# First six chunks' scores from each head's own 40 rows, the two heads of a pair by turns

## The chip, the cores and the metric

The kernel runs on one core of one Trainium2 chip. The metric is the device time of one execution in microseconds (us); lower is better. Engines are called as in the profile: PE is TensorE's matmul, PEld its weight load, DVE is VectorE, ACT is ScalarE, POOL is GpSimd, SP is SyncE, which here issues DMAs.

## The reference

A gated linear recurrence per head (batch 4, 8 heads, 768 steps, head size 40) and a feed-forward layer over all 3072 tokens:

```python
for t in range(S):
    m_new = np.maximum(f_gate[:, :, t] + m, i_gate[:, :, t])
    f_stab = np.exp(f_gate[:, :, t] + m - m_new)
    i_stab = np.exp(i_gate[:, :, t] - m_new)
    C = f_stab * C + i_stab * np.einsum('bhd,bhe->bhde', vt, kt)
    n = f_stab * n + i_stab * kt
    h_tilde = np.einsum('bhde,bhe->bhd', C, qt)
    denom = np.maximum(np.abs(np.einsum('bhd,bhd->bh', n, qt)), 1.0)
    y[:, :, t] = sigmoid(o_gate[:, :, t]) * h_tilde / denom
...
x = y.transpose(0, 2, 1, 3).reshape(3072, 320)
h = x @ w_in                                    # 320 -> 2048
g = np.maximum(h, 0) + alpha * np.minimum(h, 0)
out = g @ w_out                                 # 2048 -> 320
```

## The kernel before

**Tiling.** Each batch's 768 steps are cut into six chunks of 128, so there are 24 chunks `n` in all; two chunks make a group `g` of 256 tokens, 12 groups, and the feed-forward layer runs group by group. Inside a chunk the recurrence becomes attention-like products: scores `pS` = keys times queries, weighed by decays `E`, times values (`pH`), plus the part from the running state `C` (`pI`); the state is then updated (`pu`). The first six chunks (batch 0) work in f32, the later ones on split bf16 parts; the change touches only the first six.

**How the first six chunks' scores are made.** Queries and keys are loaded by token (`qn`, `kn`), eight heads of 64 columns each, of which 40 hold data and the rest zeros. A transpose of two heads at once (`pqk`, step `qT` for queries and `kT` for keys) puts head 2p on partitions 0 to 39 and head 2p+1 on partitions 64 to 103 (`R` is 104). ACT copies queries to `qf` (step `qc`). Keys go into `kf`, a tile with two halves (step `kc`, two copies, L329 and L330): half 0 holds only the even heads' rows and half 1 only the odd heads'; the other rows are cleared once by POOL (step `kfz`, L318 and L319). A score product then runs over all 104 rows, and the cleared rows take the other head out. The step `sc{n}{par}` does the four heads of one parity of chunk n into one bank of PSUM; `wg{n}{par}` (L1096, DVE) multiplies with the decays.

**What sets the order.** `ORDER` is a list of step names that is emitted in this order; each engine and the whole program are pinned to it. Names that matter here: `sp`/`sq` spread a row of logs over partitions (`pb`), `ex`/`ey` make decays on ACT, `v` is the product with values, `fm`/`ft` the part from the state, `ta` adds, `gr gg gx gp` gate the result into `xn`, `x` transposes it to channels, `xa`/`xd` split it into XH (ACT) and XL (DVE), `um`/`uc` update the state. `i..`, `r..`, `o..` load and split weights of the feed-forward layer (last letters: d DMA, s and x on ACT, y and j on DVE, h on ACT, l on DVE, p on POOL). `U R S G K` with group and pair are the up-product, relu, slope, high part and low part of the feed-forward layer (small `r s g` and V, N the variant for other pairs), `D` the down-product. `warm2` is a pair of filler matmuls. The later part of the program follows `PATTERN`, which does not change.

Of the kernel before, what the change touches and what calls it, by code (L numbers as in the profile page):

```python
# [8 lines left out]
F32 = mybir.dt.float32  # L9
# [8 lines left out]
def kernel(ctx: ExitStack, tc: tile.TileContext, q, k, v, i_gate, f_gate, o_gate, w_in, w_out, alpha, out):  # L18
    nc = tc.nc
    B, H, S, D = q.shape  # L20
    DM, DFF = w_in.shape
    P = 128
# [3 lines left out]
    GC = 2  # L26
# [142 lines left out]
    def weighed(n):  # L169

        b, c = divmod(n, NC)
        kd = sb.tile([P, H, D], F32, tag="kd", name=f"kd{n}")
        (nc.gpsimd if n in KDP else nc.vector).tensor_tensor(
            kd, by_token_of(n, 1), wT[:, c, b * H : (b + 1) * H].unsqueeze(2).broadcast_to([P, H, D]), ALU.mult
        )
        kds[n] = kd
# [135 lines left out]
    kpads = []

    def padded_tiles():


        for K in kpads:
            nc.gpsimd.memset(K[64:R, 0], 0.0)  # L318
            nc.gpsimd.memset(K[:64, 1], 0.0)  # L319

    def zero_states():
        for C in C_t:
            nc.gpsimd.memset(C, 0.0)

    def padded(n):
        return kpads[(n + NDIR) % 2]

    def padded_copy(K, pk):
        nc.scalar.copy(K[:64, 0], pk[:64])  # L329
        nc.scalar.copy(K[64:R, 1], pk[64:R])  # L330
# [308 lines left out]
    def row_of(g, fp, e):  # L639
# [5 lines left out]
    NDIR = 6  # L645
# [7 lines left out]
    ORDER = """warm14 dq0 Cz warm2 warm2 warm2 qT0 warm2 sca0 lf0a kT0 i00d lf0z lf0b li0 L0 sca1 bj0 dq1 warm2 qc0 lqa lqb kc0 lqc lqd sp01 eeL i00s
        lf1a lqe wt0 warm2 warm2 warm2 qT1 qc1 bTt bTc ex01 warm2 sp00 warm2 warm2 sp11 r0d lf1b ewj wTt wTc ex00 warm2
        sp10 ex11 kT1 i00y L1 li1 do0 dv0 kfz i01d eTt ex10 wd0 dq2 gma i00j sc00 o0d lpa sc01 um0 kc1 gmd gmm sc11
        eTc eel bj1 og1 r0s uc0 fm1 wtl wg01 sc10 ewl lpb i11d wd1 alT wg00 gmc qT2 i01s glt ft1 wg10 glc alC dL lpc
        lpd lpe qc2 warm2 wg11 dv1 um1 uc1 i00h i01x i01j kT2 kc2 i00p o0s o0x sp20 v0 r0y r0j gr0 sp21 fm2 dq3 ex20
        warm2 o0j r0h i01h ft2 i01p ex21 o0h warm2 gg0 r0l gx0 i11s sc20 wg20 v1 ta1 gr1 qT3 qc3 i11x gp0 x0 xa0 sc21
        dL4 gg1 gx1 gp1 kT3 wg21 x1 xa1 o1d wd3 xd0 r0H xd1 wd2 sq30 ey30 r0L i11j ex40 o0l F0 U00 i20d i10d R00 S00
        kc3 v2 ta2 um2 uc2 o1s o1y U01 dq4 i10s i10x i10j sq31 gr2 o1j i11k i11l ey31 qT4 G00 ex41 fm3 ft3 sc30 K00  # L660
        wg30 i10h um3 uc3 D00 R01 kT4 i20s do1 S01 qc4 wd4 kc4 o1h i20x sc31 wg31 dv2 um4 uc4 i20j og2 o2d i20h gg2
        i10p fm4 o1l o5d sc41 wg41 G01 K01 i21d gx2 r2d sc40 i20p o2s o2x dq5 wg40 o5s o5x v3 ta3 o2j gr3 gg3 o2h o5j
        r2s dL5 o4d r2x o2l U02 o3d r2j gx3 gp3 R02 gp2 i21s v4 ft4 ta4 qT5 qc5 r2H ex50 r2h r2p U03 x2 R03 S02 G02 x3
        dq6 i21y i21j r2L i31d fm5 ft5 xa2 xd2 i21h i21p dv3 i30d kT5 kc5 K02 S03 o4s o4y D01 G03 wd6 K03 o3s o3y o3j
        D02 do2 dL7 ex51 o7d o4j o6d U04 R04 S04 o3h xa3 V05 r05 o3p o4h sc50 o4p sc51 G04 i31s i31x xd3 s05 wg51 um6
        uc6 K04 gr4 wg50 F1 U10 U11 R10 S10 og3 gg4 gx4 dL6 gp4 R11 S11 G10 o5h o5p v5 K10 D10 U12 ta5 G11 g05 K11 vp0
        i31j i30s i30x gr5 gg5 U13 i31h i30j R12 i30h D11 S12 i31l G12 gx5 gp5 K12 D12 R13 dq7 S13 o7s i30l U06 o7x
        do3 o7j N05 G13 K13 D13 tp0 o6s tp1 o6x R06 tp2 x4 x5 o6j o6h vp1 U07 o7h tp3 D03 D04 D05 R07 S06 G06 S07 o6l
        xa5 xd5 xa4 xd4 G07 K06 K07 D06 o7l D07 Z0"""
# [271 lines left out]
    def first_group():  # L941
# [14 lines left out]
        f, i, rst, m = fi[:, 0, :S], fi[:, 1, :S], rm[:, 0, :S], rm[:, 1, : S + 1]  # L956
# [54 lines left out]
            nc.vector.tensor_copy(gates[:, GC:], ps[:, : (NC - GC) * n].rearrange("p (c a) -> p c a", a=n))  # L1011
            yield

        for j in range(2):
            kpads.append(sb.tile([P, 2, 512], F32, tag="kS", name=f"kf{j}", bufs=2))
        qk = {}

        def by_channel(n, j, copy):
            pq = psa(f"pqk{n}_{j}")
            transposed(pq, (qn_t if j == 0 else kn_t)[n % NQ])  # L1020
            yield
            if j == 0:
                qk[n] = sb.tile([P, 512], F32, tag="qf", name=f"qf{n}"), padded(n)
# [56 lines left out]

        pS = {}

        def scores(n, par):
            if n >= GC:
                ps = psa(f"pS{n}_{par}")
            elif n * par == 0:
                ps = ps_h.tile([P, 512], F32, tag="h", name=f"pS{n}_{par}")
            else:
                ps = ps_o.tile([P, 512], F32, tag="o1", name=f"pS{n}_{par}")
            for p in range(NPR):  # L1090
                sl = slice(p * P, (p + 1) * P)
                nc.tensor.matmul(ps[:, sl], qk[n][1][:R, par, sl], qk[n][0][:R, sl], start=True, stop=True)  # L1092
            pS[n, par] = ps

        def weigh(n, par):
            nc.vector.tensor_tensor(E[n, par], pS[n, par], E[n, par], ALU.mult)  # L1096
# [34 lines left out]
        steps = {}  # L1131
# [55 lines left out]
        def decay_parts(k, tag):  # L1187
# [25 lines left out]
            bj1=lambda: nc.gpsimd.tensor_tensor(bj[:, t1], li[:, t1], L[:, t1], ALU.subtract),
# [9 lines left out]
        def values_of(n):  # L1223
            got["h", n] = values(n, [E[n, 0], E[n, 1]])
# [5 lines left out]
        def chunk_steps(n):  # L1230

            steps[f"wd{n}"] = lambda: weighed(n)
            steps[f"v{n}"] = lambda: values_of(n)
            steps[f"ta{n}"] = lambda: added(n)
            steps[f"x{n}"] = lambda: x_first(n)
            add(f"xa{n} xd{n}", lazily(lambda: x_parts(n)))
            add(f"um{n} uc{n}", lazily(lambda: update_steps(n)))
            if n > 0:
                add(f"fm{n} ft{n}", lazily(lambda: state_part(n)))
            add(f"gr{n} gg{n} gx{n} gp{n}", lazily(lambda: gated_steps(n, got["T" if n else "h", n])))  # L1240
            add(f"qT{n} qc{n}", lazily(lambda: by_channel(n, 0, nc.scalar.copy)))
# [123 lines left out]
```

## Time and profile before

| what | value |
|---|---|
| median of 3 runs (lowest, highest) | 456.08 us (455.85, 456.25) |
| the profiled execution | 456.2 us, span 454.5 us, granted clock 0.998 |
| busy share PE, DVE, ACT, POOL | 99%, 68%, 69%, 69% |
| score matmuls of the first six chunks (L1092) | 96, starting between 14.2 and 67.2 us |
| copies into `kf` (L329 and L330) | 12, starting between 7.0 and 60.8 us |

The table's shares are means over the whole span. The change lies in the first 70 us or so, where the six chunks of batch 0, the gates' scans and the splitting of all weights run beside the first feed-forward products; a busy PE there includes modelled ends of matmuls, so how far apart two groups start says more than how long they are shown busy.

### The profile page before, as it was taken

The numbers are of one execution on the slowest core, as the hardware profiler recorded it, in microseconds if no ns is written. First come the engines' busy times: TensorE is split into PE (matmuls) and PEld (weight loads), VectorE is DVE, ScalarE is ACT, GpSimd is POOL, SyncE is SP. The second block draws the span as 40 slices with busy tenths as digits, with TensorE's granted clock in tenths as the row PEclk, the third lists the DMA queues.
The fourth block names the chain that finished last, engine by engine and source line by source line (L and its number), as shares of the span: only waits on it lengthen the run. The fifth ranks groups of instructions, "written<-read, shape, count | busy, mean of one in ns | idle before, by whom it ended". The sixth has DMA issues, their size and how long they took to land.

```text
span 454.5 us, 11766 instructions
## 1 busy us (share of the span) xinstructions
PE 448.2 (99%) x4418; PEld 438.8 (97%) x4418; DVE 310.9 (68%) x659; ACT 314.9 (69%) x717; POOL 312.6 (69%) x400
## 2 busy tenths in 40 slices
PE   8999999999999999999999999999999999999996
PEld 6789999999999999999999999999999999999996
DVE  4798999558866767767767767767767767753321
ACT  5999997959767767758768758658758668433331
POOL 7836566737889698588798698597798696143231
PEclk9999999999999999999999999999999999999999
DMA  8999998769674575597783783589682451000000
GB/s 182 248 253 214 232 232 226 139 143 180 156 168 110 137 160 104 133 184 163 121 183 103 131 179 105 115 188 180 128 168 86 97 142 40 1 30 1 30 1 29
DMA packets 156162, 61.60 MB, mean 136 GB/s; under 512 B 140154, under 2 KB 145834, under 8 KB 156106
## 3 DMA queue, kind: packets, MB, share of 16 engines
q1 hardware_dynamic: 156026, 60.75, 59.9%
q8 instruction: 35, 0.57, 0.5%
q14 instruction: 21, 0.17, 0.1%
q10 hardware_dynamic: 80, 0.11, 0.1%
HBM read 36.90 MB, written 4.03 MB: 90 GB/s over the span
## 4 chain that ended last, share of the span: by engine, by line
PE 91%; ACT 4%; DVE 3%; POOL 1%; issue 1%; POOLq 0%; DVEq 0%; ACTq 0%
PE po L771 36%; PE ph L734 5%; PE ph L739 5%; PE ph L735 5%; PE ph L736 5%; PE ph L741 5%; PE ph L737 5%; PE ph L740 5%; PE ph L738 5%; PE pH L390 4%; PE pS L491 4%; PE pu L192 2%; PE px L600 2%; PE pS L1092 2%; PE pH L349 2%; PE pI L415 1%
## 5 line engine op out<-in xcount | busy, mean ns | idle before, releaser
L760 POOL TENSOR_TENSOR gl<-g,gh 128x512 fp32r<-128x512 f32 x74 | 96.1, 1301 | 32.5 <-ACT gh L758 31.3
L744 ACT ACTIVATE g<-ph 128x512 f32<-128x512 f32 x96 | 57.3, 597 | 81.7 <-PE ph L741 79.7
L771 PE MATMUL po<-OH,gh 128*128 128x320 f32 x368 | 111.3, 314 | 0.0
L771 PE MATMUL po<-OL,gh 128*128 128x320 f32 x368 | 108.7, 308 | 0.0
L749 DVE SCALAR_TENSOR_TENSOR g<-g,oma,ph 128x256 f32<-128x256 f32 x148 | 63.6, 471 | 65.5 <-ACT g L744 64.1
L771 PEld LDWEIGHTS po<-OH,gh 128*128 128x128 f32 x368 | 69.2, 188 | 0.0
L771 PEld LDWEIGHTS po<-OL,gh 128*128 128x128 f32 x368 | 69.2, 188 | 0.0
L771 PE MATMUL po<-OH,gl 128*128 128x320 f32 x368 | 68.8, 308 | 0.0
L771 PEld LDWEIGHTS po<-OH,gl 128*128 128x128 f32 x368 | 57.5, 188 | 0.3 <-DVE gl L760 0.3
L734 PE MATMUL ph<-XH,WH 128*128 128x256 f32 x192 | 54.1, 282 | 0.5 <-DVE g L749 0.5
L735 PE MATMUL ph<-XH,WH 128*128 128x256 f32 x192 | 53.4, 278 | 0.0
L736 PE MATMUL ph<-XH,WL 128*128 128x256 f32 x192 | 53.2, 277 | 0.0
L739 PE MATMUL ph<-XL,WH 128*128 128x256 f32 x192 | 53.2, 277 | 0.0
L741 PE MATMUL ph<-XL,W 128*128 128x256 f32 x192 | 53.1, 277 | 0.0
L737 PE MATMUL ph<-XH,WL 128*128 128x256 f32 x192 | 53.1, 277 | 0.0
L738 PE MATMUL ph<-XH,W 128*128 128x256 f32 x192 | 53.1, 276 | 0.0
L740 PE MATMUL ph<-XL,WH 128*128 128x256 f32 x192 | 53.1, 276 | 0.0
L462 ACT ACTIVATE E<-Lb,gates 128x128 f32<-128x128 f32 x160 | 50.0, 393 | 0.0
L758 ACT CAST gh<-g 128x512 fp32r<-128x512 f32 x74 | 45.7, 618 | 4.0 <-PE po L771 2.4
L375 ACT CAST E<-pS 128x512 bf16<-128x512 f32 x72 | 41.1, 582 | 6.3 <-DVE pS L372 5.8
L465 POOL TENSOR_SCALAR_AFFINE_SELECT E<-E 128x512 f32<-128x512 f32 x40 | 27.0, 676 | 15.0 <-ACT E L462 14.4
L734 PEld LDWEIGHTS ph<-XH,WH 128*128 128x128 f32 x192 | 36.1, 188 | 0.6 <-ACT gh L758 0.6
(200 smaller groups left out, 1127.2 us busy)
## 6 DMA issues: line engine op xcount, KB each, us to landing
Lb<-L_d SPq DMA_DIRECT2D x20, 512.0 KB
wo<-in_moe_w_out_dram SPq DMA_DIRECT2D x8, 640.0 KB
wi<-in_moe_w_in_dram SPq DMA_DIRECT2D x8, 512.0 KB
qn<-in_q_dram SPq DMA_DIRECT2D x24, 160.0 KB
kn<-in_k_dram SPq DMA_DIRECT2D x24, 160.0 KB
og<-in_o_gate_dram SPq DMA_DIRECT2D x24, 160.0 KB
va<-in_v_dram SPq DMA_DIRECT2D x24, 160.0 KB
out_dram<-ob SPq DMA_DIRECT2D x11, 320.0 KB
```

The costliest lines, as they stand in the source:

```text
L734: nc.tensor.matmul(dst, WH[half][:, 0, hs], XH[:, 0], start=True, stop=False)
L735: nc.tensor.matmul(dst, WH[half][:, 1, hs], XH[:, 1], start=False, stop=False)
L736: nc.tensor.matmul(dst, WL[half][:, 0, hs], XH[:, 0], start=False, stop=False)
L737: nc.tensor.matmul(dst, WL[half][:, 1, hs], XH[:, 1], start=False, stop=False)
L738: nc.tensor.matmul(dst, W2[:, fs], XH[:, 2], start=False, stop=False)
L739: nc.tensor.matmul(dst, WH[half][:, 0, hs], XL[:, 0], start=False, stop=False)
L740: nc.tensor.matmul(dst, WH[half][:, 1, hs], XL[:, 1], start=False, stop=False)
L741: nc.tensor.matmul(dst, W2[:, fs], XL[:, 2], start=False, stop=True)
L744: nc.scalar.activation(gt, ph, AF.Relu, scale=-1.0)
L749: nc.vector.scalar_tensor_tensor(out=y[:, e], in0=gt[:, e], scalar=oma[:, f : f + 1], in1=ph[:, e], op0=ALU.mult, op1=ALU.add)
L760: (nc.vector if split else nc.gpsimd).tensor_tensor(gl, y, gh.bitcast(F32), ALU.subtract)
L771: nc.tensor.matmul(po[j], x[:, e, j * P : (j + 1) * P], W[f // NB][:, f % NB], **ends)
```

## The change

The keys are no longer padded: `kf` is used as one tile of 104 partitions, filled by one ACT copy per chunk, and the POOL clears of step `kfz` are gone. One step `sc{n}` replaces `sc{n}0` and `sc{n}1`; it takes both PSUM banks and goes through the four pairs of heads, even head (partitions 0 to 39) and odd head (partitions 64 to 103) by turns. In `ORDER` some steps around these move; one `warm2` is dropped and one moves.

```diff
-    def padded_copy(K, pk):
-        nc.scalar.copy(K[:64, 0], pk[:64])
-        nc.scalar.copy(K[64:R, 1], pk[64:R])
...
-            kpads.append(sb.tile([P, 2, 512], F32, tag="kS", name=f"kf{j}", bufs=2))
+        keys = [sb.tile([P, 2, 512], F32, tag="kS", name=f"kf{j}", bufs=2)[:, 0] for j in range(2)]
...
-                copy(qk[n][j][:R], pq[:R])
-            else:
-                padded_copy(qk[n][j], pq)
+            copy(qk[n][j][:R], pq[:R])
...
-        def scores(n, par):
-            if n >= GC:
-                ps = psa(f"pS{n}_{par}")
...
-            for p in range(NPR):
-                sl = slice(p * P, (p + 1) * P)
-                nc.tensor.matmul(ps[:, sl], qk[n][1][:R, par, sl], qk[n][0][:R, sl], start=True, stop=True)
-            pS[n, par] = ps
+        def scores(n):
+
+            for par in range(2):
+                if n >= GC:
+                    ps = psa(f"pS{n}_{par}")
...
+                pS[n, par] = ps
+            for p in range(NPR):
+                sl = slice(p * P, (p + 1) * P)
+                for par in range(2):
+                    r = slice(64 * par, 64 * par + D)
+                    nc.tensor.matmul(pS[n, par][:, sl], qk[n][1][r, sl], qk[n][0][r, sl], start=True, stop=True)
...
-        dv0 kfz i01d eTt ex10 wd0 dq2 gma i00j sc00 o0d lpa sc01 um0 kc1 gmd gmm sc11
+        dv0 i01d eTt ex10 wd0 dq2 gma i00j sc0 o0d lpa um0 kc1 gmd gmm
...
-        i11s sc20 wg20 v1 ta1 gr1 qT3 qc3 i11x gp0 x0 xa0 sc21 dL4 gg1 gx1 gp1 kT3 wg21 x1 xa1 o1d wd3 xd0 r0H xd1
+        i11s qT3 ta1 qc3 gr1 i11x sc2 x0 xa0 dL4 gg1 gx1 gp1 wg20 x1 warm2 xa1 xd0 o1d wd3 xd1 r0H wg21
```

On PE, the scores of chunk 0 in the row before (`um0`'s `pu` follows them; `x4` stands for four heads, each two passes in the trace):

```order
L1092 MATMUL pS_0_310<-qf_188,kf_131 128x128 x4
L1092 MATMUL pS_1_319<-qf_188,kf_131 128x128 x4
L192 MATMUL pu_324<-va_81,kd_304 40x42 x8
L1182 MATMUL pg<-g_gd,unit 104x192
L1092 MATMUL pS_1_339<-qf_220,kf_132 128x128 x4
```

And now:

```order
L1079 MATMUL pS_0_305<-qf_188,kf_131 128x128
L1079 MATMUL pS_1_306<-qf_188,kf_131 128x128
L1079 MATMUL pS_0_305<-qf_188,kf_131 128x128
L1079 MATMUL pS_1_306<-qf_188,kf_131 128x128
L1079 MATMUL pS_0_305<-qf_188,kf_131 128x128
L1079 MATMUL pS_1_306<-qf_188,kf_131 128x128
L1079 MATMUL pS_0_305<-qf_188,kf_131 128x128
L1079 MATMUL pS_1_306<-qf_188,kf_131 128x128
L192 MATMUL pu_319<-va_81,kd_299 40x42 x8
```

The same eight products stand there, the even and the odd head of each pair by turns. On DVE, before the first up-product, the row before from the gating of chunk 1 on (`r`, `og`, `xn`: steps `gr1`, `gg1`, `gx1`; L1096 is `wg20` and `wg21`):

```order
L1096 TENSOR_TENSOR E_0_464<-pS_0_490,E_0_464 128x512
L1228 TENSOR_TENSOR T_387<-T_387,pH_496 128x336
L436 SCALAR_TENSOR_TENSOR r_506<-T_387 128x8
L440 RECIPROCAL r_506<-r_506 128x8
L445 SCALAR_TENSOR_TENSOR og_285<-og_285,r_506 128x320
L449 TENSOR_TENSOR xn_446<-T_387,og_285 128x320
L1096 TENSOR_TENSOR E_1_477<-pS_1_527,E_1_477 128x512
L593 TENSOR_TENSOR XL_524<-p_0_518,XH_523 128x2x128
L594 TENSOR_TENSOR XL_524<-p_0_519,XH_523 128x128
L593 TENSOR_TENSOR XL_524<-p_0_518,XH_523 128x2x128
L594 TENSOR_TENSOR XL_524<-p_0_519,XH_523 128x128
```

And now:

```order
L1214 TENSOR_TENSOR T_381<-T_381,pH_475 128x336
L420 SCALAR_TENSOR_TENSOR r_497<-T_381 128x8
L424 RECIPROCAL r_497<-r_497 128x8
L429 SCALAR_TENSOR_TENSOR og_284<-og_284,r_497 128x320
L433 TENSOR_TENSOR xn_439<-T_381,og_284 128x320
L1082 TENSOR_TENSOR E_0_457<-pS_0_501,E_0_457 128x512
L577 TENSOR_TENSOR XL_517<-p_0_511,XH_516 128x2x128
L578 TENSOR_TENSOR XL_517<-p_0_512,XH_516 128x128
L577 TENSOR_TENSOR XL_517<-p_0_511,XH_516 128x2x128
L578 TENSOR_TENSOR XL_517<-p_0_512,XH_516 128x128
L1082 TENSOR_TENSOR E_1_470<-pS_1_502,E_1_470 128x512
```

Both weighings of chunk 2 have moved back, `wg20` behind the gating of chunk 1 and `wg21` behind the two XL steps that the first up-product reads. On ACT, chunk 1's keys (the copy of queries comes earlier; L1221 and L1207 are the same step `eel`), before:

```order
L1192 CAST LP<-g_L 32x256
L329 COPY kf_132<-pqk_1_277 64x512
L330 COPY kf_132<-pqk_1_277 40x512
L1221 ACTIVATE g_WH_95<-g_L 32x512
L152 ACTIVATE og_285<-og_285 128x640
```

And now:

```order
L1178 CAST LP<-g_L 32x256
L1008 COPY kf_132<-pqk_1_276 104x512
L1207 ACTIVATE g_WH_95<-g_L 32x512
L152 ACTIVATE og_284<-og_284 128x640
L815 ACTIVATE t_wr_337<-wr_249 128x512
```

One copy stands where two stood, in the same place.

More of the change, by code (lines that the diff above doesn't have):

```diff
@@ L310, in shifted @@
         chunk[n] = (Q, K, None)
[L312 to L319, printed above, removed]
     def zero_states():
@@ L323, in zero_states @@
             nc.gpsimd.memset(C, 0.0)
-    def padded(n):
-        return kpads[(n + NDIR) % 2]
-    def padded_copy(K, pk):
-        nc.scalar.copy(K[:64, 0], pk[:64])
-        nc.scalar.copy(K[64:R, 1], pk[64:R])
     def after(n):
@@ L652 @@
     FILL = {}
[L653 to L669, printed above, removed]
@@ new lines @@
+    ORDER = """warm14 dq0 Cz warm2 warm2 warm2 qT0 warm2 sca0 lf0a kT0 i00d lf0z lf0b li0 L0 sca1 bj0 dq1 warm2 qc0 lqa lqb kc0
+        lqc lqd sp01 eeL i00s lf1a lqe wt0 warm2 warm2 warm2 qT1 qc1 bTt bTc ex01 warm2 sp00 warm2 warm2 sp11
+        r0d lf1b ewj wTt wTc ex00 warm2 sp10 ex11 kT1 i00y L1 li1 do0 dv0 i01d eTt ex10 wd0 dq2 gma i00j sc0 o0d
+        lpa um0 kc1 gmd gmm eTc eel bj1 og1 r0s uc0 fm1 wtl wg01 sc1 ewl lpb i11d wd1 alT wg00 gmc qT2 i01s glt
+        ft1 wg10 glc alC dL lpc lpd lpe qc2 warm2 wg11 dv1 um1 uc1 i00h i01x i01j kT2 kc2 i00p o0s o0x sp20 v0
+        r0y r0j gr0 sp21 fm2 dq3 ex20 o0j r0h gg0 i01h ft2 i01p gx0 ex21 v1 gp0 o0h r0l i11s qT3 ta1 qc3 gr1
+        i11x sc2 x0 xa0 dL4 gg1 gx1 gp1 wg20 x1 warm2 xa1 xd0 o1d wd3 xd1 r0H wg21 wd2 r0L i11j ex40 o0l F0 U00
+        i20d i10d kT3 sq30 R00 S00 kc3 ey30 v2 ta2 um2 uc2 o1s o1y U01 dq4 i10s i10x i10j sq31 gr2 o1j i11k i11l
+        ey31 qT4 G00 ex41 fm3 ft3 qc4 K00 i10h um3 uc3 D00 R01 kT4 i20s do1 S01 wd4 kc4 o1h i20x sc3 wg30 wg31
+        dv2 um4 uc4 i20j og2 o2d i20h gg2 i10p fm4 o1l o5d sc4 wg41 G01 K01 i21d gx2 r2d i20p o2s o2x dq5 wg40
+        o5s o5x v3 ta3 o2j gr3 gg3 o2h o5j r2s dL5 o4d r2x o2l U02 o3d r2j gx3 gp3 R02 gp2 i21s v4 ft4 ta4 qT5
+        qc5 r2H ex50 r2h r2p U03 x2 R03 S02 G02 x3 dq6 i21y i21j r2L i31d fm5 ft5 xa2 xd2 i21h i21p dv3 i30d kT5
+        kc5 K02 S03 o4s o4y D01 G03 wd6 K03 o3s o3y o3j D02 do2 dL7 ex51 o7d o4j o6d U04 R04 S04 o3h xa3 V05 r05
+        o3p o4h o4p sc5 G04 i31s i31x xd3 s05 wg51 um6 uc6 K04 gr4 wg50 F1 U10 U11 R10 S10 og3 gg4 gx4 dL6 gp4
+        R11 S11 G10 o5h o5p v5 K10 D10 U12 ta5 G11 g05 K11 vp0 i31j i30s i30x gr5 gg5 U13 i31h i30j R12 i30h D11
+        S12 i31l G12 gx5 gp5 K12 D12 R13 dq7 S13 o7s i30l U06 o7x do3 o7j N05 G13 K13 D13 tp0 o6s tp1 o6x R06
+        tp2 x4 x5 o6j o6h vp1 U07 o7h tp3 D03 D04 D05 R07 S06 G06 S07 o6l xa5 xd5 xa4 xd4 G07 K06 K07 D06 o7l
+        D07 Z0"""
@@ L1012, in all_by_token @@
             yield
-        for j in range(2):
-            kpads.append(sb.tile([P, 2, 512], F32, tag="kS", name=f"kf{j}", bufs=2))
+        keys = [sb.tile([P, 2, 512], F32, tag="kS", name=f"kf{j}", bufs=2)[:, 0] for j in range(2)]
         qk = {}
@@ L1022, in by_channel @@
             if j == 0:
-                qk[n] = sb.tile([P, 512], F32, tag="qf", name=f"qf{n}"), padded(n)
-                copy(qk[n][j][:R], pq[:R])
-            else:
-                padded_copy(qk[n][j], pq)
+                qk[n] = sb.tile([P, 512], F32, tag="qf", name=f"qf{n}"), keys[(n + NDIR) % 2]
+            copy(qk[n][j][:R], pq[:R])
             yield
@@ L1081, in first_group @@
         pS = {}
-        def scores(n, par):
-            if n >= GC:
-                ps = psa(f"pS{n}_{par}")
[L1086 to L1089, printed above, removed]
+        def scores(n):
+            for par in range(2):
+                if n >= GC:
+                    ps = psa(f"pS{n}_{par}")
+                elif n * par == 0:
+                    ps = ps_h.tile([P, 512], F32, tag="h", name=f"pS{n}_{par}")
+                else:
+                    ps = ps_o.tile([P, 512], F32, tag="o1", name=f"pS{n}_{par}")
+                pS[n, par] = ps
             for p in range(NPR):
                 sl = slice(p * P, (p + 1) * P)
-                nc.tensor.matmul(ps[:, sl], qk[n][1][:R, par, sl], qk[n][0][:R, sl], start=True, stop=True)
-            pS[n, par] = ps
+                for par in range(2):
+                    r = slice(64 * par, 64 * par + D)
+                    nc.tensor.matmul(pS[n, par][:, sl], qk[n][1][r, sl], qk[n][0][r, sl], start=True, stop=True)
         def weigh(n, par):
@@ L1216, in first_group @@
             eeL=lambda: nc.scalar.activation(eL[:, P:GT], L[:, P:GT], AF.Exp),
-            kfz=padded_tiles, Cz=zero_states,
+            Cz=zero_states,
             og1=lambda: open_gate(0, 0, GC), og2=lambda: open_gate(0, GC, 2 * GC), og3=lambda: open_gate(0, 2 * GC, NC),
@@ L1232, in chunk_steps @@
             steps[f"wd{n}"] = lambda: weighed(n)
+            steps[f"sc{n}"] = lambda: scores(n)
             steps[f"v{n}"] = lambda: values_of(n)
@@ L1248, in chunk_steps @@
                 add(f"ex{n}{par}", lazily(lambda par=par: decay(n, par)))
-                steps[f"sc{n}{par}"] = lambda par=par: scores(n, par)
                 steps[f"wg{n}{par}"] = lambda par=par: weigh(n, par)
```

## The prediction

> **What bounds the kernel now.** I read the page first, then busy time by stretches, then the chain of waits, then the waits of single engines. The profiled run took 456.2 us with a span of 454.5 us; the median of the runs is 456.08 us, so what is won in the span is taken off 456.08.
>
> ```profile
> PE 448.2 (99%) x4418; PEld 438.8 (97%) x4418; DVE 310.9 (68%) x659; ACT 314.9 (69%) x717; POOL 312.6 (69%) x400
> ...
> PE 91%; ACT 4%; DVE 3%; POOL 1%; issue 1%; POOLq 0%; DVEq 0%; ACTq 0%
> ```
>
> TensorE is the bound on average, but the change touches only the start. The stretches below are cut where the first feed-forward matmul begins (32.4 us) and where the last stall of TensorE in the start ends (68.4 us).
>
> ```profile
> 14.20:32.40 18.20, 17.91 (x177) 16.04 (x177) 15.40 (x36) 16.95 (x40) 10.59 (x15) 1.00 0.97 264
> 32.40:48.40 16.00, 16.00 (x174) 15.30 (x172) 14.35 (x31) 15.08 (x36) 9.57 (x12) 1.00 0.93 223
> 48.40:68.40 20.00, 19.54 (x176) 19.02 (x174) 19.33 (x37) 19.17 (x40) 12.66 (x12) 1.00 0.99 230
> 68.40:110.00 41.60, 41.57 (x362) 41.31 (x363) 30.49 (x60) 31.79 (x69) 25.63 (x33) 1.00 0.79 178
> 110.00:454.50 344.50, 340.90 (x3456) 338.00 (x3454) 224.27 (x485) 222.83 (x514) 242.55 (x302) 1.00 0.51 112
> ```
>
> Columns after the length are PE, PEld, DVE, ACT, POOL, clock, DMA share, GB/s. Up to 68.4 us four resources are nearly full at once: PE 98 to 100%, DVE 85, 90 and 97%, ACT 93, 94 and 96%, DMA 93 to 99%. Behind 68.4 us only PE is full (DVE 73%, then 65%), so whatever time is won by 68.4 us is kept to the end. The clock is full throughout and plays no part. The chain of waits says who gates that point:
>
> ```profile
> 60.78 0.58 ACT kf L330
> ...
> 61.39 0.81 ACT t_wo L830
> ...
> 62.22 0.76 DVE t_wo L846
> ...
> 67.81 0.48 DVE g L749
> ...
> 68.43 0.36 PE ph L734
> ```
>
> It runs over ACT (through the second copy of a chunk's keys) and then 6 us of DVE before PE goes on. So between 48 and 68 us TensorE time alone is worth little; DVE's 49.08 us of work in the 54.2 us from 14.2 to 68.4 are the floor, and its 5.12 us of idle time the most that can be won.
>
> **Part 1: the score matmuls.** Each logical f32 product is two passes here.
>
> ```profile
> 7.04 1.15 PE L1038 MATMUL pb<-g_L,ident 32*128 32x128 f32 x8
> ...
> 14.22 2.05 PE L1092 MATMUL pS<-qf,kf 104*128 104x128 f32 x16
> 16.20 0.51 PE L192 MATMUL pu<-va,kd 128*40 128x42 f32 x16
> 16.64 0.57 PE L1182 MATMUL pg<-g_gd,unit 32*104 32x192 f32 x2
> ...
> 17.13 1.16 PE L1092 MATMUL pS<-qf,kf 104*128 104x128 f32 x8
> 18.13 1.02 PE L409 MATMUL pI<-C,qf 104*128 104x84 f32 x8
> ...
> 46.53 1.99 PE L1092 MATMUL pS<-qf,kf 104*128 104x128 f32 x16
> 48.35 1.88 PE L349 MATMUL pH<-va,E 128*128 128x42 f32 x16
> ```
>
> From start to next start sixteen score passes take 1.82 us (46.53 to 48.35), 0.114 each; with the rows at 14.22 and 17.13 it is 0.124 and 0.125 with the waits at their ends. Eight passes over 32 rows (7.04) last 1.15 us, as eight over 104 rows do (17.13, 1.16). So 40 rows instead of 104 save nothing by themselves, and sixteen passes of `pH`, which stream 42 columns where `pS` streams 128, last nearly as long (1.88 against 1.99): the 128 stationary columns set the pace. The one thing that can help is that two heads at different partitions run at once. The trace has no matmuls that alternate between row ranges. Its nearest row is `pu`, whose heads alternate between output partitions 0 and 64: sixteen passes of 40 stationary columns in 0.44 us (16.20 to 16.64), 27 ns each, where 40/128 of 114 ns would be 36 one after the other; with the first and last passes' latency inside the 0.44, the steady pace is about half of the serial one. The bounds for a chunk's sixteen passes are 0.9 us (full overlap, half of 1.82) and 1.82 us (none), or more if turns cost. I take 0.95, near the row of `pu`, since it is the same array, type and kind of turn, only across columns.
>
> Entering and leaving such a group has a price; the row of `pu` shows the leaving:
>
> ```profile
> 36.48 0.51 PE L192 MATMUL pu<-va,kd 128*40 128x42 f32 x16
> 36.92 0.38 PE L734 MATMUL ph<-XH,WH 128*128 128x256 f32 x1
> 37.14 0.29 PE L735 MATMUL ph<-XH,WH 128*128 128x256 f32 x1
> 37.27 0.28 PE L736 MATMUL ph<-XH,WL 128*128 128x256 f32 x1
> ```
>
> The first `ph` behind it takes 0.22 us to the next one, which then takes 0.13: 0.09 us. I book 0.05 to 0.1 on either side, so a chunk costs about 1.1 us. Per chunk 1.95 (mean of 1.82 and the two halves with their latencies) less 1.1 is 0.85, and over six chunks 5.1 us of TensorE time.
>
> The Trainium skill ("TensorEngine Tiling (Array Packing)", Tiling Modes, Key Properties) says that a change of tiling mode, not of the tile alone, drains the engine. The 0.09 us behind `pu` agrees in kind; by that rule the turns inside a chunk cost nothing and only the twelve entries and exits count, which is what I booked. The skill's "TensorE: Matmul & The Clock Gate" (Part 3, Measured speedup vs the span model) gives 3.07 times for four row tiles; an estimate from its share of four, 0.77, for two tiles is 1.82/1.54 = 1.18 us a chunk instead of 0.95, and the TensorE sum would be 3.7 us; no run here shows it.
>
> **Part 2: keys copied once.**
>
> ```profile
> L329 ACT COPY kf<-pqk x6: 570/580/587, 7.0 to 60.2; 64x512 f32<-64x512 f32 x6
> L330 ACT COPY kf<-pqk x6: 581/581/581, 7.6 to 60.8; 40x512 f32<-40x512 f32 x6
> ```
>
> One copy of 104 partitions replaces two; a copy's time here does not depend on its partitions (64 and 40 cost the same), so ACT loses six times 0.58, 3.5 us. The first (chunk 0) is worth nothing: ACT then waits for POOL at 8.3 us anyway. Five, 2.9 us, lie in the full stretches.
>
> **Part 3: no padding.** Four POOL clears go.
>
> ```profile
> 13.30 0.69 POOL L318 MEMSET kf<- 40x512 f32 x1
> ...
> 15.18 0.52 POOL L319 MEMSET kf<- 64x512 f32 x1
> 15.67 1.39 POOL L1213 TENSOR_TENSOR g_WH<-g_li,g_L 32x512 f32<-32x512 f32 x1
> ```
>
> `bj1` (L1213), behind them, can start up to 1 us sooner, limited by the scan that ends about 14.7. POOL is 58% busy there, so this feeds the later gates (`glt`), not the path directly.
>
> **Part 4: moved steps.** Scores of both parities become ready together; `v1` and the gating of chunk 0 come ahead of `sc2`, `wg21` (0.69 us of DVE) behind the XL steps, the transpose `kT3` and spread `sq30` behind the first up-product, one filler pair (0.22 us) is gone, and `sc3` stands behind `kT4`. No DVE work is removed. Of what is behind a moved step: `wg30` waits until `sc3`, but its reader `v3` comes after `sc4`, 3 us on; `wg21` is read by `v2`, behind `U00`. I cost these at nothing; if that cover is gone, `wg21`'s 0.69 us is the price. The order of the DMAs in SP's queue stays what it was.
>
> **The sum, taken on DVE.** These are the named waits of DVE from 14.2 to 68.4 us:
>
> ```profile
> DVE C L224 <- PE pu L192: 0.7, 1, 0.7
> DVE t_wi L852 <- ACT wi L840: 0.7, 2, 0.4
> DVE C L229 <- POOL C L217: 0.6, 1, 0.6
> DVE E L1096 <- PE pS L1092: 0.4, 1, 0.4
> DVE gates L1011 <- PE ps_g_all L1007: 0.4, 1, 0.4
> DVE T L1228 <- PE pH L349: 0.4, 1, 0.4
> DVE E L1096 <- PE pqk L273: 0.2, 1, 0.2
> DVE t_wo L846 <- ACT t_wo L830: 0.2, 1, 0.2
> DVE T L420 <- PE pI L409: 0.2, 1, 0.2
> ```
>
> On PE 2.3 us, on ACT 0.9, on POOL 0.6. Up to 32.4 us PE sheds 3 times 0.85 and ACT 1.2, so nearly all of the 2.3 goes; I take 2.0. Of ACT's 0.9 I take 0.7, since ACT is 2.9 us lighter by then. POOL's 0.6 stays. That is 2.7 us; I take 0.4 off for what comes late next, DMA: its idle share up to 68.4 us is 0.03 of 18.2, 0.07 of 16.0 and 0.01 of 20.0, together 1.9 us, and beyond that loads only use up the time by which they landed early. The gain is 2.3 us, and 456.08 - 2.3 = 453.8 us (span about 452.2). TensorE's other 2.8 us turn into more waiting for DVE ahead of 68 us.
>
> **Rivals.**
> - *No overlap.* Weight loads of the two heads go one after the other, a chunk stays at 1.8 to 2.0 us. For it: the pace is set by stationary columns, and both heads use all 128; against it: `pu`. Then only ACT's part is left: 0.7 less small change, 455.5.
> - *Everything passes.* Waits of DVE vanish altogether and its 1.2 us of unnamed gaps shrink too: 5.1 us of TensorE time against 5.12 of DVE idle, at most 451.0, likelier 451.6. Against it: POOL's and DMA's rows.
> - *DMA becomes the bound.* At share 0.99 from 48 us on, the loads of weights cannot follow, and ACT and DVE wait for them: gain 0.9, time 455.2.
> - *Slower.* Each turn between partitions 0 and 64 empties the array, at the 0.09 us of the row behind `pu`: eight turns a chunk add 0.7 and twelve entries the rest, so a chunk costs 2.6 us, 0.65 more than now, 3.9 in all; PE has 0.3 + 0 + 0.5 us idle to hide it, and ACT's gain does not help PE: about 3, 459. It decides from 1.95 us a chunk upward. Against it: the sixteen turns in `pu` cost no such thing.
>
> **How the numbers follow.** Forecast 56% (452.6 to 455.0 by its bounds), no overlap 13%, everything passes 9%, DMA 13%, slower 9%. About 0.2%, 0.9 us, is what measurement tells from no change here. Faster than 455.2: all of the first and third, half of DMA, a third of no overlap, 76%. Same: the rest of these two, 15%. Slower 9%. Eight in ten: forecast, everything passes, DMA and a part of no overlap, 451.2 to 455.8.
>
> **What would show it.** Right: `pS` passes in close pairs, a chunk about 1.1 us from its start to the next group; first `ph` at about 30.5 us instead of 32.46; the waits of DVE on `pu`, `pS` and `pH` gone; the `ph` now at 68.43 near 66.1, with a longer PE stall ahead of it; everything behind it shifted alike. ACT shows six copies into `kf`. Wrong: `pS` passes 0.11 us apart; ACT or DVE waiting for DMA of `wr`, `wo` or `wi` around 50 to 62 us; or the lead at 32 us gone by 68.

## Result and profile after

The changed kernel took 460.31 us (median of 5 runs, 459.93 to 460.88) against 456.08 us before: 1.0094 times the time, interval 1.008 to 1.0109. It is 4.2 us slower, where 2.3 us faster was forecast. The profiled execution shown here took 460.51 us with a span of 458.6 us. Times are medians over every execution, and the ratios leave out one execution each of three kernels below (e1 465.92, e5 466.22, f2 467.66 us) that ran at a lower clock than the others; without these the three medians are 457.75, 459.35 and 460.13 us.

The page and the busy time by stretches, cut again where the first `ph` begins (35.8 us, before 32.5) and where the first part ends (72.9 us, before 68.4); columns as in the prediction:

```profile
PE 448.9 (98%) x4416; PEld 437.4 (95%) x4416; DVE 311.7 (68%) x659; ACT 310.6 (68%) x711; POOL 310.2 (68%) x396
...
PEclk9789999999999999999999999999999999999999
```

```profile
14.20:35.80 21.60, 18.49 (x167) 15.64 (x165) 16.56 (x35) 15.22 (x37) 9.75 (x12) 0.76 0.85 236
35.80:53.70 17.90, 17.74 (x192) 16.27 (x192) 15.65 (x33) 14.59 (x35) 9.66 (x12) 1.00 0.85 201
53.70:72.90 19.20, 17.54 (x161) 16.70 (x160) 18.79 (x36) 17.82 (x38) 12.13 (x12) 1.00 0.92 229
72.90:114.40 41.50, 41.50 (x362) 41.21 (x363) 30.47 (x60) 31.61 (x69) 25.54 (x33) 1.00 0.77 172
```

The loss is all in the first 73 us: 3.3 us by the first `ph`, 1.2 more by 72.9; the next 41.5 us take what they took. Two things were not there before: the clock is 0.76 in the first stretch, and DVE's work from 14.2 us to the end of the first part is 16.56 + 15.65 + 18.79 = 51.0 us, where it was 49.08. DMA's share is lower than before (0.85, 0.85 and 0.92 against 0.97, 0.93 and 0.99), so it is not the bound.

**The score passes did what was forecast.** Timeline of PE, start and duration in us, with the idle time ahead of the group in brackets:

```profile
13.99 1.16 PE L1079 MATMUL pS<-qf,kf 40*128 40x128 f32 x16
15.08 0.51 PE L192 MATMUL pu<-va,kd 128*40 128x42 f32 x16
17.92 0.93 PE L1168 MATMUL pg<-g_gd,unit 32*104 32x192 f32 x2 [2.33 <-DVE gates L985]
18.78 2.00 PE L393 MATMUL pI<-C,qf 104*128 104x84 f32 x8
```

From their start to the next group, `pu`, sixteen passes take 1.09 us (1.1 was forecast, 1.98 before at this place). What was won, 0.9 us, is followed by a wait of 2.33 us that did not exist. The timelines of DVE and POOL at that place say why:

```profile
14.88 1.77 DVE L839 SCALAR_TENSOR_TENSOR t_wi<-wi,t_wi 128x512 uint32<-128x512 uint32 x1
16.59 1.19 DVE L1161 TENSOR_TENSOR g_gd<-ident,gam 32x192 f32<-32x192 f32 x1
17.70 0.17 DVE L985 COPY gates<-ps_ge 128x32 f32<-128x32 f32 x1
...
14.71 1.40 POOL L1199 TENSOR_TENSOR g_WH<-g_li,g_L 32x512 f32<-32x512 f32 x1 [1.56 <-DVE g_L L1134]
16.19 1.37 POOL L973 TENSOR_TENSOR g_WL<-g_WH,g_L 32x512 f32<-32x512 f32 x1
```

and the two DVE instructions in the kernel before:

```profile
14.97 0.67 DVE L854 SCALAR_TENSOR_TENSOR t_wi<-wi,t_wi 128x512 uint32<-128x512 uint32 x1
15.58 0.34 DVE L1175 TENSOR_TENSOR g_gd<-ident,gam 32x192 f32<-32x192 f32 x1
```

Without the four clears POOL's `bj1` (first POOL row) starts at 14.71 instead of 15.67, 0.17 us ahead of DVE's `i00j` (first DVE row), and the next POOL operation follows at 16.19. The two DVE instructions, each with two SBUF operands, end 0.54 and 0.22 us after the POOL instruction beside them and take 1.77 and 1.19 us instead of 0.67 and 0.34: 1.95 us more. `gates`, which the PE pass waits for, is copied at 17.70 instead of 15.85.

The Trainium skill ("SBUF — State Buffer", "SBUF: two separate sides") has the rule: a DVE operation with two SBUF inputs and a GpSimd operation that reads SBUF take a shared pair of ports as an exclusive lock, for the whole instruction, and the first to start has it. The rows agree: 1.77 us, ending 0.54 us behind the POOL row. A clear reads nothing, and `i00j` ran beside clears in 0.67 us in the kernel before.

The clock, by stretches:

```profile
16.40:20.00 3.60, 2.08 (x8) 1.63 (x8) 3.55 (x8) 3.20 (x6) 3.21 (x4) 0.54 0.82 200
20.00:23.40 3.40, 3.40 (x23) 2.99 (x23) 1.13 (x3) 0.00 (x0) 0.80 (x2) 0.50 1.05 301
23.40:26.90 3.50, 3.50 (x30) 2.80 (x29) 2.26 (x7) 1.70 (x4) 1.27 (x1) 0.50 0.99 203
26.90:30.30 3.40, 3.40 (x34) 3.19 (x33) 2.51 (x7) 3.40 (x9) 0.00 (x0) 1.00 0.99 337
```

It is 0.5 for 10.2 us from 16.7 us on. While it is, eight `pI` passes take 2.00 us instead of 1.02, DVE waits 3.5 us for PE (below), and ACT 4.4 us for the transposes of chunk 2's queries and 1.1 for those of its keys:

```profile
DVE E L1082 <- PE pS L1079: 1.5, 1, 1.5
DVE gates L996 <- PE ps_g_all L992: 1.2, 1, 1.2
DVE T L404 <- PE pI L393: 0.8, 1, 0.8
```

### The profile page after: what moved, and what is told of

Read it like the earlier page. It is cut to its first block, busy times and chain, and to the rows that moved or that the text cites. A ratio compares the mean times of both kernels' runs of the same rounds, so it can differ in the third digit from the quotient of the medians.

```text
span 458.6 us, 11749 instructions
## 1 busy us (share of the span) xinstructions
PE 448.9 (98%) x4416; PEld 437.4 (95%) x4416; DVE 311.7 (68%) x659; ACT 310.6 (68%) x711; POOL 310.2 (68%) x396
## 4 chain that ended last, share of the span: by engine, by line
PE 84%; DVE 4%; issue 3%; POOL 3%; ACT 3%; DMA 1%; SPq 1%; POOLq 0%; DVEq 0%; ACTq 0%
PE po L756 36%; PE ph L719 5%; PE ph L720 5%; PE ph L721 4%; PE ph L726 4%; PE ph L722 4%; PE ph L725 4%; PE ph L724 4%; PE ph L723 4%; PE pH L374 4%; PE pS L475 4%; PE px L584 2%; PE pI L399 1%; DMA wi<-in_moe_w_in_dram 1%; PE pu L192 1%
## 5 line engine op out<-in xcount | busy, mean ns | idle before, releaser
L745 POOL TENSOR_TENSOR gl<-g,gh 128x512 fp32r<-128x512 f32 x74 | 96.0, 1299 | 32.5 <-ACT gh L743 31.3
```

The costliest lines, as they stand in the source:

```text
L745: (nc.vector if split else nc.gpsimd).tensor_tensor(gl, y, gh.bitcast(F32), ALU.subtract)
```

## The experiments

Every kernel below computes the whole reference. The kernel before ran beside each set: 456.03 us beside e1, e2, e3 and e5, 456.15 beside the f kernels, 456.06 beside the g kernels, 456.11 beside the h kernels; all times are medians.

**e1_clears: the changed kernel with POOL's clears put back** at their old place and size, on the half of the key tiles that nothing reads.

```
- dv0 i01d        + dv0 kfz i01d
```

> The changed kernel with four POOL clears of the old sizes put back at the old place, on a half of the key tiles that nothing reads. Theory A (without the clears POOL's bj1 starts 1 us sooner, at 14.7 us, and holds up DVE's i00j and gmd, so that PE waits 2.3 us for pg's bank and its clock falls to half for 10 us): i00j takes about 0.7 us again instead of 1.77, the wait for pg shrinks to about 0.4 us, the clock stays full, and the time is 453 to 455 us. Rival C (the moved steps around sc2 and the first up-product lose the time): still about 459 us or more. Rival D (the alternating passes lower the clock by themselves): the clock falls as before, 459 us.

457.88 us (ratio 1.0043, 1.0031 to 1.0056), where 453 to 455 was expected: 2.4 us of the loss are gone. The meeting is gone too:

```profile
14.66 0.67 DVE L822 SCALAR_TENSOR_TENSOR t_wi<-wi,t_wi 128x512 uint32<-128x512 uint32 x1
15.27 0.34 DVE L1151 TENSOR_TENSOR g_gd<-ident,gam 32x192 f32<-32x192 f32 x1
15.53 0.17 DVE L968 COPY gates<-ps_ge 128x32 f32<-128x32 f32 x1
```

But the clock still falls, twice, and the second time after 3.4 us in which PE was busy throughout:

```profile
16.40:23.30 6.90, 6.86 (x51) 6.01 (x51) 3.66 (x8) 4.62 (x9) 4.54 (x7) 0.51 0.98 265
...
47.20:50.60 3.40, 3.40 (x33) 3.01 (x33) 3.32 (x8) 1.83 (x5) 1.39 (x2) 1.00 1.15 237
50.60:54.00 3.40, 3.40 (x18) 3.40 (x18) 3.33 (x8) 3.29 (x5) 1.74 (x2) 0.50 0.46 130
```

So the wait of 2.33 us is not what lets the clock fall, or not alone. It falls in every execution of e1, the fastest too (granted clock over the whole run 0.993 at most).

**e2_filler: the changed kernel with 18 filler passes** where PE waits for `gates`.

```
- um0 kc1         + um0 warm18 kc1
```

> The changed kernel with 18 filler matmuls (about 2 us) between pu of chunk 0 and pg, where PE now idles 2.3 us; the clears stay out and DVE stays late. It parts the cost of the late DVE from that of the half clock. Theory A with the clock as the larger part: the clock stays at 1.0, pI of chunk 1 takes 0.9 us instead of 1.95, the late DVE (1.9 us) stays, and the time is 454.5 to 457 us. Were the late DVE itself the larger part: 458 us or more with a full clock. Rival D: the clock falls all the same.

457.28 us (457.00 to 461.25; ratio 1.0044, 1.0021 to 1.0068). In the profile the clock holds up to 50.5 us, falls there for 3.4 us, and DVE meets POOL as in the changed kernel. So the meeting and the clock are two losses: 3.0 of the 4.2 us come back with the meeting still there. Two of the six executions had a granted clock of 0.999 and 1.0 and took 457.11 and 457.00 us: at full clock the meeting leaves about 1.0 us over the kernel before. The two losses overlap, since e1, which took away the meeting alone, brought back 2.4.

**e3_before_bj1: the kernel before with `bj1` moved ahead**, so that it starts at 14.67 us, and the second tile's clears behind it.

```
- um0 kc1 ... eel bj1 og1        + um0 bj1 kfy kc1 ... eel og1
```

> The kernel before, with the clears of the second key tile put behind bj1 in POOL's order, so that bj1 starts about 1 us sooner, at 14.7 us; scores, copies and all other steps as before. Theory A: DVE's i00j becomes about 1 us longer (1.7 instead of 0.67), the waits of PE on DVE between 15 and 18 us grow, and the time is 0.5 to 1.5 us longer than before, or 3 to 4 us if the clock falls too. Rival C: no change, 456.1 us.

456.72 us (ratio 1.0015, 1.0002 to 1.0027), clock 1.0.

```profile
14.84 1.76 DVE L843 SCALAR_TENSOR_TENSOR t_wi<-wi,t_wi 128x512 uint32<-128x512 uint32 x1
16.53 0.34 DVE L1164 TENSOR_TENSOR g_gd<-ident,gam 32x192 f32<-32x192 f32 x1
16.80 0.17 DVE L989 COPY gates<-ps_ge 128x32 f32<-128x32 f32 x1
```

The same 1.1 us on `i00j`, in a kernel that has none of the rest of the change: so an earlier `bj1` alone does it. It costs 0.7 us at the end.

**e5_no_turns: e1 with four even heads first, then four odd.**

```
-for p in range(NPR):
-    for par in range(2):
+for par in range(2):
+    for p in range(NPR):
```

> As the first kernel here (changed, clears put back), but the four even heads first and then the four odd heads, so that passes on the same partitions follow each other. If the turns are what lets passes overlap, sixteen passes take 1.8 us and more instead of 1.1, and the time is 1.5 to 3 us above that of the kernel with turns. If 40 rows alone were enough: no difference.

460.08 us (ratio 1.0082, 1.0068 to 1.0096). The profile is of the execution of 466.22 us, with the clock at 0.5 for 24 us from 18.9 us on, so only its first rows, at full clock, are used:

```profile
13.96 1.71 PE L1069 MATMUL pS<-qf,kf 40*128 40x128 f32 x16
15.60 0.51 PE L192 MATMUL pu<-va,kd 128*40 128x42 f32 x16
```

1.64 us for sixteen passes without turns, 1.09 with: the turns save, 1.5 times by the group. The starts of single passes in the traces say how. With turns the passes of the two heads start 0.007 us apart, and such a pair every 0.112 us (changed kernel, from 14.20 us on). Passes on the same partitions follow each other at 0.112 us too, 40 rows or 104 (f1). So two heads do run at once, at twice the pace, and what keeps the group from half the time is its first and last pass, some 0.2 us each, which it has with and without turns. Without turns the trace has two chains of eight passes, each at that pace, and the second starts at 14.516 us, with three passes of the first still to come: part of the work overlaps even so, and that is where 1.64 instead of f1's 1.98 us comes from, not the fewer rows.

**f1_rows104: the same order of steps, but padded keys, two copies and 104 rows**, as in the kernel before.

```
-r = slice(64 * par, 64 * par + D)
-nc.tensor.matmul(pS[n, par][:, sl], qk[n][1][r, sl], qk[n][0][r, sl], ...)
+nc.tensor.matmul(pS[n, par][:, sl], qk[n][1][:R, par, sl], qk[n][0][:R, sl], ...)
```

> The changed kernel's order of steps, but the keys padded as in the kernel before: two copies per chunk's parity, four clears on POOL, and score passes over 104 rows. Theory D (passes over 40 rows, with their lower use of the array, are what lets the granted clock fall): the clock stays at 0.998 or more, and the time is that of the kernel before plus the 1.1 us that the moved steps cost in the second stage, 456.5 to 457.5 us, with the first ph pass near 32.5 us. Rival (the order of the steps, or the total of TensorE's busy time, lets it fall): the clock falls to 0.5 from some 16.5 us on here too, and the time is 458 to 460 us.

458.37 us (ratio 1.005, 1.0037 to 1.0062), and the clock is full:

```profile
PEclk9999999999999999999999999999999999999999
```

Both halves teach. The clock falls with 40 rows (e5, same order, same clears: 0.985 to 0.989 in its three other executions) and not with 104 (0.999 to 1.0 in all five). The two kernels also differ in the copies of the keys and in how long a group keeps PE at work, so what of the shorter passes counts for the clock is not parted. And with the old passes the order of steps, joined score steps included, costs 2.2 us, twice what was expected.

Half of these 2.2 us is DVE's own work: from 14.2 us to U10's first pass (70.7 us) DVE is busy 50.25 us where it was 49.08, and idle 6.25 where it was 5.12. The longest new piece is a second meeting with POOL; f1's rows, then the same two before:

```profile
27.94 1.70 DVE L834 TENSOR_TENSOR W<-t_wr,W 64x512 fp32r<-64x512 f32 x1
27.82 1.28 POOL L834 TENSOR_TENSOR WL<-t_wi,WH 128x512 fp32r<-128x512 f32 x1 [4.10 <-ACT WH L830]
...
27.13 0.69 DVE L866 TENSOR_TENSOR W<-t_wr,W 64x512 fp32r<-64x512 f32 x1
27.42 1.54 POOL L866 TENSOR_TENSOR WL<-t_wi,WH 128x512 fp32r<-128x512 f32 x1 [4.11 <-ACT WH L862]
```

Before, DVE came first and took 0.69 us; in f1 POOL comes 0.12 us ahead, and DVE takes 1.01 us more.

**f2_masks: `sq30 ey30` ahead of `r0L` again.**

```
- wd2 r0L ... kT3 sq30 R00 S00 kc3 ey30 v2        + wd2 sq30 ey30 r0L ... kT3 R00 S00 kc3 v2
```

> The changed kernel with one thing undone: sq30 and ey30 stand ahead of r0L again, as in the kernel before. Theory C (these two, moved behind the first U step, make POOL's masks late for the state's scaling): from the first ph pass to the pass group of U10 it takes 36.0 us again rather than 37.1, and the time is 459.2 us (1.1 less than the changed kernel), the clock and the wait for the gates as in the changed kernel. Rival (their place costs nothing): 460.3 us, the stage still at 37.1.

460.16 us (1.0088, 1.0072 to 1.0103), the second stage 36.8 us: no difference from the changed kernel that can be measured at this clock; 459.2 us was expected.

**f3_clears_fill: e1 and fillers** that hold the clock.

```
- um0 kc1 ... fm1 wtl wg01 sc1 ewl        + um0 warm4 kc1 ... fm1 warm2 wtl wg01 sc1 warm4 ewl
-FILL = {}                                +FILL = {3: 6}
```

> The changed kernel with POOL's clears put back (so bj1 starts as late as in the kernel before) and more filler passes on TensorE between um0 and kc1, fm1 and sc1, and in the third chunk. If the meeting of bj1 with i00j and the fallen clock are the two losses of the first stage: clock 0.998 or more, i00j 0.67 us, first ph pass at 30.5 to 31.8 us, and the time 455 to 456.5 us, the second stage's loss of 1.1 us still in it. Rival (the first stage has a third loss, or the fillers cost their own time): first ph at 32.5 us or later, and 457 us or more.

456.17 us (1.0002, 0.9993 to 1.0011), clock 1.0, first `ph` at 31.4 us. **f4_all** is f3 with f2's order:

> The kernel with clears and fillers put back, and sq30 and ey30 ahead of r0L as before. If the three losses (meeting of POOL and VectorE, the clock, the moved masks) are all there is: first ph pass at 30.5 to 31.8 us, 36.0 us from there to U10, and the time 453.5 to 455.5 us, which is what was forecast for the change. Rival (what was gained ahead of the first U step is lost in the second stage whatever the order): the second stage takes 37 us, and the time is 456 us or more.

455.88 us (0.9994, 0.9986 to 1.0003), clock 0.999. Faster than the changed kernel by 4.4 us; against the kernel before not to be told apart. Against f3, with full clock in both, the masks' old place is worth 0.3 us (455.70 to 455.97 against 456.01 to 456.28, eleven executions each): a small price of a moved step, which f2 could not show. The first `ph` is at 31.4 us, 1.1 ahead of before, but U10's first pass, the `ph` that stood at 68.4, only 0.4 ahead; the second stage takes 36.7 us, between the 36.0 of the theory and the 37 of the rival. DVE's lead is gone sooner still, f4's row first, then the one before:

```profile
34.80 1.25 DVE L834 TENSOR_TENSOR OL<-t_wo,OH 128x640 fp32r<-128x640 f32 x1
...
34.80 1.25 DVE L866 TENSOR_TENSOR OL<-t_wo,OH 128x640 fp32r<-128x640 f32 x1
```

It starts at the same time. Of the 1.1 us, 0.68 was no lead: `wg21` now stands behind the XL steps that the first `ph` reads, and is only put off. A `t_wi` at 33.87 us, which takes 1.01 us instead of 0.69 beside a POOL mask that started before it, uses up the rest. The longest waits of DVE in f4, from 14.2 to 72 us, and the place of the first:

```profile
DVE C L229 <- POOL C L217: 1.2, 1, 1.2
DVE gates L979 <- PE ps_g_all L975: 0.9, 1, 0.9
DVE E L1072 <- PE pS L1069: 0.6, 1, 0.6
```

```profile
41.15 0.68 DVE L728 TENSOR_TENSOR gl<-ph,gh 128x512 fp32r<-128x512 f32 x1
43.07 0.67 DVE L229 TENSOR_TENSOR C<-C,pu 40x168 f32<-40x168 f32 x2 [1.24 <-POOL C L217]
```

In the kernel before, the weighing `wg30` stood in that gap:

```profile
41.67 0.68 DVE L760 TENSOR_TENSOR gl<-ph,gh 128x512 fp32r<-128x512 f32 x1
42.27 0.68 DVE L1096 TENSOR_TENSOR E<-pS,E 128x512 f32<-128x512 f32 x1
43.55 0.67 DVE L229 TENSOR_TENSOR C<-C,pu 40x168 f32<-40x168 f32 x2 [0.60 <-POOL C L217]
```

POOL scales the state of chunk 3 only behind a mask that waits for ACT; DVE comes there earlier now and waits longer, since the weighing that filled 0.68 us of the gap has been moved behind it. DMA's share is 0.99 from 31.4 to 68.1 us in f4, but no engine is shown waiting for a DMA there.

**g1_order_late and g2_order_early: f3's passes, clears and fillers in the order of the kernel before**, each chunk's two score steps joined at the place of the later or of the earlier one.

```
g1: - sc20 wg20 v1 ... xa0 sc21 / sc30 K00 wg30 ... sc31 wg31    + v1 ... xa0 sc2 wg20 / K00 ... sc3 wg30 wg31
g2: - sc20 wg20 v1 ... xa0 sc21 / sc30 K00 wg30 ... sc31 wg31    + sc2 wg20 v1 ... xa0 / sc3 K00 wg30 ... wg31
```

> The score passes over 40 rows by turns, one copy of the keys, clears and fillers as in f3, but the steps in the order of the kernel before; the two score steps of a chunk are one step at the place of the later of the two, and the weighing of its even heads right behind it. Theory M (the moved steps cost 2.2 us, what f1 lost with the old passes, and the new passes and the single copy win 2.2 us, what f3 gains over f1): first ph pass at 30.5 to 31.4 us, the second stage 35 to 36 us, and the time 453.5 to 454.5 us. Rival N (the loss in f1 comes of both parities being one step, wherever it stands): 456 us or more, the second stage 36.5 us or longer.

> As g1, but the one score step at the place of the earlier of the two, and the weighing where it was. Theory M: 453.5 to 454.5 us here as well. If the scores' place matters by itself (what comes behind TensorE's shorter group has to wait for VectorE), the earlier place is better than the later one by up to 0.7 us, the longest wait that the f4 run shows behind a score group. Rival N: 456 us or more.

457.90 us (1.0053, 1.0039 to 1.0066) and 456.71 us (1.0018, 1.001 to 1.0027), the second stage 36.6 and 36.3 us. The clock fell in three of the five executions of g1 (0.991 to 0.995) and in four of the eleven of g2 (0.996, the profiled one among them); the others took 457.46 and 457.69 us, and 456.31 to 456.75. Theory M falls all the same: the old order does not bring the gain back. In g1, at full clock, the first `ph` is at 33.1 us, 1.7 later than in f3 (0.7 of it `wg21`, which f3 puts off), and the second stage 0.5 shorter: the moved steps win ahead of the first `ph` and lose behind it. f1, g1 and g2 have the joined score step in common, and also DVE's `W` behind POOL's `WL` (1.70, 1.65 and 1.65 us, against 1.24 in f3 and 0.69 before); neither was tried alone. One cost looks like that of the joined step: chunk 4's sixteen passes take 1.55 us in f4 and 1.58 in the changed kernel instead of 1.09, with only two passes started in the first 0.5 us and pairs from then on, as if one of the two banks were not yet free; this was not followed up.

**h1_scale: f4 with POOL's scaling of chunk 3's state ahead of the mask.**

```
- i11l ey31       + i11l mu3 ey31
```

> The f4 kernel with POOL's scaling of the state of chunk 3 issued ahead of the mask ey31 instead of behind it. Theory P (VectorE's work sets the pace up to U10, and its 1.2 us wait for this scaling, which the weighing wg30 shortened to 0.6 us in the kernel before because it stood ahead of it, is part of what the moved steps cost): the wait goes, the second stage is shorter by up to 1.2 us, and the time is 454.7 to 455.4 us. Rival (behind it the next late thing is as late, TensorE or ScalarE): less than 0.3 us, 455.6 us or more.

456.39 us (1.0004, 0.9996 to 1.0013). The wait of 1.24 us is gone, and the time is 0.5 us worse than f4's:

```profile
38.42 1.26 DVE L827 SCALAR_TENSOR_TENSOR t_wi<-t_wi,wi 128x512 uint32<-128x512 uint32 x1
...
40.61 1.12 DVE L841 TENSOR_TENSOR WL<-t_wi,WH 128x512 fp32r<-128x512 f32 x1
...
45.34 1.29 DVE L1079 TENSOR_TENSOR E<-pS,E 128x512 f32<-128x512 f32 x2 [0.85 <-PE pS L1076]
```

```profile
38.12 0.99 POOL L199 TENSOR_TENSOR C<-C,gamB 104x336 f32<-104x336 f32 x1 [0.88 <-DVE C L236]
40.05 1.14 POOL L1055 TENSOR_SCALAR_AFFINE_SELECT E<-E 128x512 f32<-128x512 f32 x1 [0.93 <-ACT E L1046]
```

POOL's moved scaling (38.12) and the mask behind it (40.05) each start just ahead of a DVE instruction, and these two take 1.26 and 1.12 us where f4 has 0.68 and 0.69; then DVE waits 0.85 us for the scores. The rival was right in its time, and in its reason for a part: up to U10 DVE is idle only 3.96 us (4.65 in f4), but busy 50.54 (49.25).

**h2_scale_gates: h1 with fewer fillers ahead of chunk 1's scores and the gates' transposes earlier.**

```
- fm1 warm2 wtl wg01 sc1 warm4 ... gmc qT2 i01s glt ft1        + fm1 wtl wg01 sc1 warm2 ... gmc warm2 glt warm2 qT2 i01s ft1
```

> h1, and in the first stage two waits of VectorE shortened: fewer fillers ahead of chunk 1's scores, and the transposes of the second tile's gates (glt) ahead of chunk 2's queries, where the f4 run shows VectorE waiting 0.6 us for the score group and 0.9 us for these gates. Theory P (what VectorE no longer waits is won at the end): another 0.5 to 1.3 us, 453.5 to 454.8 us. Rival (VectorE's lead ahead of the first ph pass is lost again by 35 us, as f4's lead over the kernel before was): no better than h1 by more than 0.2 us. If the fewer fillers let the clock fall, the granted clock in the first stage shows it and the time is above 456 us.

456.79 us (1.002, 1.0011 to 1.0029). The profile has clock 1.0, but with four of the fillers at later places the clock fell in five of the eleven executions (0.991 to 0.993, 457.19 to 457.87 us); the other six took 456.56 to 456.79. DVE's wait for the gates is 0.5 instead of 0.9 us, and the first `ph` is at 31.7 instead of 31.4: nothing won at full clock either. DVE's idle time fell again, to 3.71 us, and its work rose to 51.09.

## Why the prediction was wrong

Each kernel against the one before that ran beside it:

| kernel | us over before | what is in it | step |
|---|---|---|---|
| f1_rows104 | +2.2 | steps joined and moved | +2.2 |
| f3_clears_fill | 0.0 | and 40 rows by turns, one copy, fillers | -2.2 |
| e1_clears | +1.9 | without the fillers: the clock falls | +1.8 |
| changed kernel | +4.2 | without the clears: POOL meets DVE | +2.4 |

In another order of undoing, the steps of the clock and of the meeting would share the 4.2 us otherwise (e2). The steps of f1 and f3 hold other meetings of DVE and POOL as well: DVE's work up to U10 is 49.08 us before, 50.25 in f1, 49.25 in f3 and 51.00 in the changed kernel.

- **Right: parts 1 and 2.** At full clock a chunk's scores cost 1.09 us (chunk 4's excepted), and by the mechanism forecast, two heads at once; ACT copies keys once, six times (L1008, 0.59 us); DMA did not become the bound. f3 is 2.2 us faster than f1, near the forecast gain of 2.3, but that is no proof of the sum: half of it is DVE's work, 1.0 us shorter by other meetings, and in the old order (g1, g2) no gain appears. "Slower" was among the rivals at about 459 us; its reason, turns that empty the array, is not what happened.
- **Failed: part 3**, "feeds the later gates, not the path directly". An engine that starts sooner was costed as a gain or nothing. POOL's `bj1` and the POOL operation behind it keep DVE, the engine on which the sum was made, for 1.1 and 0.85 us longer, 1.95 us together. At the end the first alone costs 0.7 us (e3) and both about 1.0 (e2's executions at full clock). The rest of the 2.4 us goes, as far as the profiles show, with a clock that in this stretch stays down for 10.2 us instead of 6.9; that was not tried by itself. The Trainium skill's rule on shared ports, named above, was there to be weighed against the rows of `bj1` and `i00j`, and the prediction did not.
- **Failed: "The clock is full throughout and plays no part."** True of the kernel before; the change replaced passes over 104 rows by passes over 40. f1 against e5 shows that the clock falls with the 40-row passes and not with the old ones, e1 against f3 that the fall costs 1.8 us. That a wait makes it fall, my first reason, is refuted by e1's second fall. The Trainium skill ("TensorE: Matmul & The Clock Gate", Part 1: The HAM clock gate) puts the fall down to a window of about 3.4 us in which TensorE is idle; here it fell behind 3.4 us of full busy time (47.20:50.60), so a busy PE in the profile is not enough.
- **Failed: part 4**, "I cost these at nothing". The moved and joined steps cost 2.2 us in f1, about half as longer work of DVE (1.17) and half as more idle time (1.13). Three pieces are seen. DVE's `W` meets POOL's `WL`, 1.01 us. `wg30`, said to have 3 us to spare because its reader comes later, was itself the cover of DVE's wait for POOL: the slack of its reader was looked at and not the gap that it filled. And the masks' later place is 0.3 us (f4 against f3). How much of the 2.2 us is owed to joining the score steps and how much to moving steps stays open, g1 and g2 having brought back neither.
- **Failed: the sum.** It took 2.0 of DVE's 2.3 us of waits for PE as gone. In f4, with every other loss cured, 1.5 us of such waits are left (gates 0.9, scores 0.6) and POOL's grew from 0.6 to 1.2; DVE's idle time up to U10 went from 5.1 to 4.65 us (53.9 less 49.25 busy), not to 2.8. And the sum held DVE's work fixed at 49.08 us: h1 and h2 did take the idle time down to 3.96 and 3.71 us, and the work grew to 50.54 and 51.09, with the instructions that lie beside POOL. What else would come late next the sum had only for DMA.

## What to carry to other kernels

Removing an instruction from an engine that is not the bound moves everything behind it on that engine: look at what the neighbours do in the new place, and where a DVE operation of two SBUF operands would start just behind a POOL operation that reads SBUF, count what is left of the POOL instruction as lost on DVE (1.1 us of 1.40 and 0.85 of 1.37 here). An engine's busy time is therefore no fixed floor: compare it, not only the waits, in every variant. A step that moves away uncovers the wait that it filled, so ask of a moved step what stood still beside it, not only when its reader comes. Before making matmuls smaller, ask whether what is left still holds the clock, and have fillers at hand to tell a clock loss from a wait.

## What the hardware did that was not expected

- The granted clock fell to 0.5 in steps of about 3.4 us (10.2 us in the changed kernel, 6.9 and 3.4 in e1), once straight behind 3.4 us of full PE time made of short f32 passes, 40-row scores among them. Sixteen more filler passes in the first 50 us held it at 0.998 to 1.0 in all eleven executions of f3; with four of them in other places (h2) it fell in five of eleven.
- Two heads at partitions 0 and 64 by turns start their passes 0.007 us apart, a pair every 0.112 us, the pace of one pass over 40 or 104 rows alone; with its first and last pass the group is 1.5 times as fast as without turns (1.09 against 1.64 us). Without turns the second chain of passes still starts ahead of the last three of the first (e5).
